# A mixture-of-experts kernel after linear attention: TensorE's order in the second expert job written by hand

## The chip, the cores and the metric

The kernel runs on one core of one Trainium2 chip. A core has five engines with instruction queues of their own: TensorE (PE in the profile; its weight loads are PEld), VectorE (DVE), ScalarE (ACT), GpSimd (POOL) and SyncE (SP, which here only issues transfers). Sixteen DMA engines move data between the device memory and the on-chip memories SBUF and PSUM. The metric is the time of one execution on the device in microseconds (us), the median of several runs.

## The reference, cut to what matters

```python
f = 1.0 / (1.0 + np.exp(-f_logit))                    # q, k, v, f_logit: 4 x 8 x 768 x 48
for t in range(S):
    state = f[:, :, t, :, None] * state + np.einsum('bhd,bhe->bhde', k[:, :, t], v[:, :, t])
    y[:, :, t] = np.einsum('bhd,bhde->bhe', q[:, :, t], state)
x = np.ascontiguousarray(y.transpose(0, 2, 1, 3)).reshape(B * S, H * D)   # 3072 x 384
...
probs = softmax(x @ w_gate); expert_idx = np.argmax(x @ w_gate, axis=1)   # 8 experts, 768 places each
h = np.maximum(np.einsum('ecd,edf->ecf', disp, w1), 0.0)                  # w1: 8 x 384 x 1024
y = np.einsum('ecf,efd->ecd', h, w2)                                      # w2: 8 x 1024 x 384
out[i] = gate_w[i] * y[expert_idx[i], pos[i]]
```

Each of the 3072 rows of the attention's result goes through the two weight matrices of one expert, with a Relu between, and is scaled by its gate.

## The kernel before, in words

**Stages.** Up to about 150 us the attention runs in slots, and its rows are written, sorted by expert, to a table `disp` in device memory. Then follow nine *jobs*, each a number of rows through the weights of one expert. Job 0, here the *first job* (256 rows of expert 0), has its first products inside the slots, and its second products are TensorE's last work there. The *second job* takes the 224 left-over rows of expert 0, with the same weights (`wsets[0]`). The *third job* is the largest of the other experts (448 rows, weights `wsets[1]`); the fourth to ninth follow by size (424, 408, 392, 376, 360 and 352 rows).

**A job.** Rows, weights and hidden values are held as a high part and a low part (`xh`/`xl`, `w1h`/`w1l`, `hh`/`hl`; `x0h`/`x0l` for the second job), since TensorE multiplies rounded fp32: each product is high·high + high·low + low·high. The *first products* (`hidden`, L758) run over the 8 tiles `ft` of 128 hidden columns, and for each over 3 slices `c` of 128 input columns: 9 matmuls per `ft`, 72 per job. ScalarE takes Relu into `hh` (L764), VectorE the rest into `hl` (L765). The *second products* run, for rows in blocks `kb` of 128, over `ft` with 3 matmuls each (`ffn2_rows`, L1019; jobs two and three, and the last ones) or with weights and rows exchanged (`ffn2`, L1253). For the second job that is two blocks, 48 matmuls. ScalarE scales the result by the gate into `yo` (L1023) and GpSimd scatters it to the output (L330).

**Rows turned.** Rows arrive as `xg` (rows on partitions) and must be turned. For jobs two and three TensorE does it: `prep_second` (L1137, two transposes per slice) and `prep` (L1223, four per slice). For the later ones `columns` copies the rows into planes (GpSimd L1193, ScalarE L1194), four transposing transfers follow (L1197), and `prep_columns` puts them together (GpSimd L1206, ScalarE L1207, L1211, VectorE L1212).

**Weights.** An expert's weights come in seven pieces, three of `w1` (512 KB each) and four of `w2` (384 KB), through three buffers `raw` (L123, L129). ScalarE copies a piece to the high part (L136); VectorE, or GpSimd for the `w2` of the third job, subtracts for the low part (L145). A buffer is free again after that.

**Gates.** `gates` (L989 to L1004) works out each row's gate and its place in the output: some nine small VectorE operations and two on ScalarE.

**What sets the order.** Each engine runs its queue in order. In the attention part TensorE's order is written out by hand (`manual_schedule`), the first job's second products with it; hooks there put `prep_second` between them, its third slice after the last `ft`. Then a flag (`slow_wide`, L1495) is read on every engine and a branch taken (L1496); behind it, in `sorted_jobs`, a scheduler sets the order of all engines from its own estimates, the program's order and a few hints (`issue_after`: not ahead of that instruction in program order). SyncE's queue holds: three pieces of `w1` of the third job; its rows `xg` (which wait until the filling rows, `disp<-zero,fill_at`, are in `disp`); its four pieces of `w2`; the fourth job's rows; the fourth job's `w1`; and so on.

## Time and profile before

| | |
|---|---|
| three runs | 372.09, 373.45, 375.27 us |
| median | 373.45 us |
| profiled execution, own time | 371.12 us |
| its span (first to last instruction) | 369.4 us |
| TensorE busy | 352.4 us, 95% of the span |
| VectorE, ScalarE, GpSimd busy | 243.7, 221.9, 168.0 us |

The profile is of one execution. Its times count from the start of the span; 1.7 us of its own time lie outside. A busy TensorE is not a TensorE at its peak: its instructions are pipelined, so the distance between two starts is its pace, and the length of one is longer than that.

### The profile page before, as it was taken

The page shows a single profiled execution, that of the slowest core. Times are in us where ns is not written, and L with a number is a line of the kernel's source. Part 1 is how long each engine was busy: PE and PEld are TensorE (multiplying, and loading weights), DVE is VectorE, ACT ScalarE, POOL GpSimd, SP SyncE. Part 2 cuts the span into 40 slices and gives each one's busy share as a digit, 9 for nine tenths or more (in the row PEclk, how much of TensorE's full clock was granted, in tenths as well). Part 3 has the DMA queues.
Part 4 walks back from the last instruction along what each step waited for, and adds up shares of the span by engine and source line. Part 5 has one row for each costly group of instructions (what it writes and reads, how often), then busy time and mean ns, then how long its engine had stood idle before and what let it go on. Part 6 is the DMA issues. An engine that isn't in the chain of part 4 may idle for free. (4 is left out here: it accounts for less than half of the span.)

```text
span 369.4 us, 10094 instructions
## 1 busy us (share of the span) xinstructions
PE 352.4 (95%) x3895; PEld 331.3 (90%) x3895; DVE 243.7 (66%) x538; ACT 221.9 (60%) x457; POOL 168.0 (45%) x282
## 2 busy tenths in 40 slices
PE   7899999999999999949999999999999999999994
PEld 6799888888888889848999899999999999999993
DVE  4998998978998947652385387566955857570310
ACT  3466667876876653435377585749749678491311
POOL 6765545774867673516503530305517326133012
PEclk9999999999999999998999999999999999999999
DMA  7999999989785432564646989798599798821001
GB/s 170 187 218 215 235 220 240 225 220 267 174 228 147 140 110 88 200 205 146 231 112 202 226 251 204 250 208 277 160 210 280 184 215 263 162 95 66 14 23 42
DMA packets 110569, 67.53 MB, mean 183 GB/s; under 512 B 92995, under 2 KB 105052, under 8 KB 110512
## 3 DMA queue, kind: packets, MB, share of 16 engines
q1 hardware_dynamic: 106784, 56.74, 62.5%
q0 software_dynamic: 3456, 9.96, 7.4%
q8 instruction: 32, 0.52, 0.6%
q14 instruction: 25, 0.20, 0.2%
q10 hardware_dynamic: 272, 0.10, 0.1%
HBM read 49.26 MB, written 11.21 MB: 164 GB/s over the span
## 5 line engine op out<-in xcount | busy, mean ns | idle before, releaser
L330 POOL DMA_INDIRECT out_dram<-yo,g_ti x29 | 30.6, 1056 | 59.1 <-ACT yo L1023 35.1
L438 POOL TENSOR_SCALAR_AFFINE_SELECT AT<-AT 128x512 f32<-128x512 f32 x48 | 29.5, 640 | 19.5 <-ACT AT L436 19.5
L1019 PE MATMUL psM<-w2h,hh 128*128 128x384 f32 (+3 forms) x112 | 37.9, 339 | 0.0
L1019 PE MATMUL psM<-w2l,hh 128*128 128x384 f32 (+3 forms) x112 | 37.5, 338 | 0.0
L1019 PE MATMUL psM<-w2h,hl 128*128 128x384 f32 (+3 forms) x112 | 37.4, 337 | 0.0
L136 ACT ACTIVATE w2h<-raw 128x768 fp32r<-128x768 f32 x32 | 26.9, 843 | 13.6 <-DMA raw<-in_moe_w_dram 13.5
L1253 PE MATMUL psM<-hh,w2h 128*128 128x424 f32 (+3 forms) x96 | 33.1, 345 | 0.0
L1253 PE MATMUL psM<-hh,w2l 128*128 128x424 f32 (+3 forms) x96 | 33.0, 344 | 0.0
L1253 PE MATMUL psM<-hl,w2h 128*128 128x424 f32 (+3 forms) x96 | 33.0, 344 | 0.0
L390 DVE TENSOR_TENSOR_SCAN Suf<-psF,direv 112x511 f32<-112x511 f32 x24 | 29.0, 1210 | 3.7 <-PE psF L370 3.7
L436 ACT ACTIVATE AT<-psA 128x512 f32<-128x512 f32 x48 | 26.4, 613 | 7.5 <-PE psA L430 3.4
L145 DVE TENSOR_TENSOR w2l<-raw,w2h 128x768 fp32r<-128x768 f32 x28 | 27.4, 980 | 4.8 <-ACT w2h L136 4.1
L145 DVE TENSOR_TENSOR w1l<-raw,w1h 128x1024 fp32r<-128x1024 f32 x21 | 26.9, 1282 | 5.3 <-ACT w1h L136 5.1
L1273 POOL COPY yo<-yq 128x384 uint16<-128x384 uint16 (+4 forms) x15 | 13.0, 915 | 36.8 <-DMA yq<-yp 36.8
L330 POOL DMA_INDIRECT disp<-rows,ri x24 | 24.9, 1036 | 10.0 <-issue 3.7
L404 DVE TENSOR_TENSOR_SCAN Rq<-psF,d 112x512 f32<-112x512 f32 x24 | 29.4, 1224 | 0.0
L136 ACT ACTIVATE w1h<-raw 128x1024 fp32r<-128x1024 f32 x24 | 25.2, 1056 | 6.1 <-DMA raw<-in_moe_w_dram 6.0
L430 PE MATMUL psA<-qT,kT 48*128 48x128 f32 x384 | 27.5, 280 | 0.6 <-DVE qT L419 0.6
L765 DVE SCALAR_TENSOR_TENSOR hl<-psA,hh 128x224 fp32r<-128x224 f32 (+8 forms) x26 | 13.8, 532 | 20.7 <-ACT hh L764 19.6
L563 ACT ACTIVATE rows<-psA 128x384 f32<-128x384 f32 x24 | 11.8, 492 | 24.6 <-PE psA L547 19.0
L526 PE MATMUL psY<-AT,ld_v 128*48 128x128 f32 (+1 forms) x384 | 26.0, 273 | 0.0
L430 PEld LDWEIGHTS psA<-qT,kT 48*128 48x128 f32 x384 | 24.1, 189 | 1.2 <-ACT kn L461 0.7
(258 smaller groups left out, 1023.9 us busy)
## 6 DMA issues: line engine op xcount, KB each, us to landing
raw<-in_moe_w_dram SPq DMA_DIRECT2D x24, 512.0 KB
raw<-in_moe_w_dram SPq DMA_DIRECT2D x32, 384.0 KB
ld_kq<-in_k_dram SPq DMA_DIRECT2D x24, 192.0 KB
ld_kq<-in_q_dram SPq DMA_DIRECT2D x24, 192.0 KB
ld_v<-in_v_dram SPq DMA_DIRECT2D x24, 192.0 KB
ld_f<-in_f_logit_dram SPq DMA_DIRECT2D x11, 384.0 KB
xg<-disp SPq DMA_DIRECT2D x4, 589.5 KB
xg<-disp SPq DMA_DIRECT2D x5, 393.0 KB
```

The costliest lines, as they stand in the source:

```text
L136: return nc.scalar.activation(hi, raw, AF.Copy)
L145: engine.tensor_tensor(lo[cs], raw[cs], hi[cs].bitcast(F32), op=ALU.subtract)
L330: ins = nc.gpsimd.indirect_dma_start(out=dst, out_offset=bass.IndirectOffsetOnAxis(ap=idx, axis=0), in_=rows, in_offset=None, bounds_check ...
L390: nc.vector.tensor_tensor_scan(out=_view(Suf[:R], m - 1, [[-1, m]]), data0=_view(F, m, [[-1, m]]), data1=_view(direv[:R], m - 1, [[-1, m]] ...
L404: nc.vector.tensor_tensor_scan(out=Rq[:R], data0=F, data1=d1[:R], initial=0.0, op0=ALU.mult, op1=ALU.max)
L430: nc.tensor.matmul(pas[s][:, p], kTs[n][r, p], qTs[n][r, p], start=True, stop=True)
L436: nc.scalar.activation(AT[:, s], pas[s], AF.Copy)
L438: nc.gpsimd.affine_select(AT[:, s], AT[:, s], pattern=[[0, NP], [1, C]], compare_op=ALU.is_ge, fill=0.0, base=0, channel_multiplier=-1)
L526: nc.tensor.matmul(py[b][64 * g : 64 * g + m, a, :], vt[:, 2 * p + s, :m], AT[:, s, p, :], start=(first(n) and a == 0), stop=(a == NP // 2 ...
L765: nc.vector.scalar_tensor_tensor(out=hl[:, :T], in0=ph[:, :T], scalar=0.0, in1=hh[:, :T].bitcast(F32), op0=ALU.max, op1=ALU.subtract)
L1019: nc.tensor.matmul(py[:n], x[:, ks], a[:, ft], start=(ft == 0 and m == 0), stop=(ft == FT - 1 and m == 2))
L1253: nc.tensor.matmul(pys[c][:, :T], a[:, ft, cs], x[:, :T], start=(ft == 0 and n == 0), stop=(ft == FT - 1 and n == 2))
```

## The change

It writes TensorE's order in the second job by hand, in a new function `second_job`, and moves what stands around it:

- The third slice of the second job's own rows is turned inside the branch, after the first three `ft` have had their products of slice 0 (27 of the 72 first products now run slice by slice over three tiles).
- The three `w1` splits of the third job stand behind the evictions `hh` of `ft` 2, 3 and 5; the second job's gates, before ahead of the branch, behind `ft` 4, in a pool of their own.
- All 72 first products run before the third job's rows are turned; the three turns (four transposes each) stand in the second row block of the second products, behind `ft` 1, 3 and 5.
- The third job's gates and the four `w2` splits (high parts on ScalarE, low parts on GpSimd) are issued behind the last turn.
- `yo` keeps its three buffers in this job, and its scatters no wait for the fills (`fills=False`). The fourth job's rows are asked for behind the second job in program order. SyncE's queue holds the same transfers in the same order.

```diff
--- before.py
+++ after.py
@@ -1006,7 +1006,7 @@
 
     out_ins, filling = [], []
 
-    def ffn2_rows(wt, hs, pr, T, fpool, hooks=None):
+    def ffn2_rows(wt, hs, pr, T, fpool, hooks=None, fills=True):
         w1h, w1l, w2h, w2l = wt
         gate, ti = pr[2:]
         for kb in range(-(-T // P)):
...
@@ -1136,18 +1134,15 @@
             for kb in range(T_FIRST[0] // P):
                 nc.tensor.transpose(pt[:, kb * P : (kb + 1) * P], xg0[:, kb, c * P : (c + 1) * P], ident)
             act = nc.scalar.activation(x0h[:, c], pt, AF.Copy)
-            with tc.issue_after(filling[0]):
-                dve = nc.vector.tensor_tensor(x0l[:, c], pt, x0h[:, c].bitcast(F32), op=ALU.subtract)
-        if c == DT - 1:
-            with tc.issue_after(act.ins), tc.issue_after(dve.ins):
-                pr1.extend((x0h, x0l) + gates(xg0, T_FIRST[0] // P, w0pool))
+            with tc.issue_after(filling[0]) if c < DT - 1 else ExitStack():
+                nc.vector.tensor_tensor(x0l[:, c], pt, x0h[:, c].bitcast(F32), op=ALU.subtract)
 
     row_loads = []
     load_second()
     with tc.manual_schedule(engines={mybir.EngineType.PE}):
         with tc.issue_after(marks["rank"].ins):
             ffn2_rows(
-                wsets[0], hs0, (None, None) + g0, T_FIRST[0], h0pool, {(0, 3): order_experts, (1, 6): lambda: prep_second(0, 1), (1, 7): lambda: prep_second(2)}
+                wsets[0], hs0, (None, None) + g0, T_FIRST[0], h0pool, {(0, 3): order_experts, (1, 6): lambda: prep_second(0, 1)}
             )
 
     actx.close()
@@ -1165,6 +1160,7 @@
         row_loads.clear()
         fpool = fctx.enter_context(tc.tile_pool(name="fpool", bufs=2, reuse_waits="tile"))
         hpool = fctx.enter_context(tc.tile_pool(name="hpool", bufs=1, reuse_waits="tile"))
+        spool = fctx.enter_context(tc.tile_pool(name="spool", bufs=1))
         rawpool = fctx.enter_context(tc.tile_pool(name="rawpool", bufs=3, reuse_waits="tile"))
         wpool = fctx.enter_context(tc.tile_pool(name="wpool", bufs=1, reuse_waits="tile"))
         wsets[1:] = [weight_tiles(wpool)]
@@ -1216,15 +1212,61 @@
             nb = -(-T // P)
             xh = fpool.tile([P, DT, TMAX], F32R, name="xh", bufs=1)
             xl = fpool.tile([P, DT, TMAX], F32R, name="xl", bufs=1)
-            for c in range(DT):
+            acts = []
+
+            def turn(c):
                 pt = psT.tile([P, 4 * P], F32, name="psT")
                 for kb in range(nb):
                     n = min(P, T - kb * P)
                     nc.tensor.transpose(pt[:, kb * P : kb * P + n], xg[:n, kb, c * P : (c + 1) * P], ident[:n, :n])
-                act = nc.scalar.activation(xh[:, c, :T], pt[:, :T], AF.Copy)
-                dve = nc.vector.tensor_tensor(xl[:, c, :T], pt[:, :T], xh[:, c, :T].bitcast(F32), op=ALU.subtract)
-            with tc.issue_after(act.ins), tc.issue_after(dve.ins):
-                gate, ti = gates(xg, nb, fpool)
+                acts.append(nc.scalar.activation(xh[:, c, :T], pt[:, :T], AF.Copy).ins)
+                acts.append(
+                    nc.vector.tensor_tensor(xl[:, c, :T], pt[:, :T], xh[:, c, :T].bitcast(F32), op=ALU.subtract).ins
+                )
+
+            return xh, xl, turn, acts
+
+        def second_job(pieces):
+            T = jobs[1][1]
+            pools = (psA, "psA"), (psM, "psM")
+            tile = lambda ft: pools[ft % 2][0].tile([P, TMAX], F32, name=pools[ft % 2][1])
+            pieces2, hs, begun = [], [], [tile(ft) for ft in range(3)]
+            w1h, w1l = wsets[0][:2]
+            for c in range(DT):
+                if c == 1:
+                    prep_second(2)
+                for ft, ph in enumerate(begun):
+                    fs = slice(ft * P, (ft + 1) * P)
+                    for n, (a, x) in enumerate(((w1h, x0h), (w1h, x0l), (w1l, x0h))):
+                        nc.tensor.matmul(
+                            ph[:, :T], a[:, c, fs], x[:, c, :T], start=(c == 0 and n == 0), stop=(c == DT - 1 and n == 2)
+                        )
+            for ft in range(FT):
+                if ft < len(begun):
+                    ph = begun[ft]
+                else:
+                    ph = tile(ft)
+                    hidden(wsets[0], x0h, x0l, T, ft, ph)
+                hs.append(hidden_out(ph, T, ft, hpool, TMAX))
+                if ft in (2, 3, 5):
+                    with tc.issue_after(hs[ft][2]):
+                        split_piece(pieces.pop(0), nc.vector)
+                    pieces2.append(weight_piece(wsets[jobs[2][2]], expert(2), rawpool, DT + len(pieces2)))
+                if ft == 4:
+                    with tc.issue_after(hs[ft][2]):
+                        gate, ti = gates(xg0, T_FIRST[0] // P, spool)
+            xg, T1 = xgs.pop(2), jobs[2][1]
+            pieces = pieces2
+            xh, xl, turn, acts = prep(xg, T1)
+            ffn2_rows(
+                wsets[0], hs, (None, None, gate, ti), T, fpool, {(1, 2 * c + 1): lambda c=c: turn(c) for c in range(DT)}, False
+            )
+            with tc.issue_after(acts[-2]), tc.issue_after(acts[-1]):
+                gate, ti = gates(xg, len(range(0, T1, P)), fpool)
+                for n in range(FT // 2):
+                    if n == len(pieces):
+                        pieces.append(weight_piece(wsets[jobs[2][2]], expert(2), rawpool, DT + n))
+                    split_piece(pieces[n], nc.gpsimd)
             return xh, xl, gate, ti
 
         def ffn1(wt, pr, T, hook, later, pools):
@@ -1286,13 +1328,8 @@
         yp = fpool.tile([P, DT, 2, 4 * P], U16, name="yp", bufs=1)
         nc.gpsimd.memset(yp[:, :, :, min(sizes[j - 2] for j in range(2, NE + 1) if j not in IN_ROWS) :], 0)
         xgs, made = {}, {}
-        for n in range(DT + FT // 2):
-            if n == DT:
-                xgs[2] = load_rows(expert(2), jobs[2][1])
-            with tc.issue_after(row_loads[-1]) if row_loads else ExitStack():
-                split_piece(weight_piece(wsets[jobs[2][2]], expert(2), rawpool, n), nc.vector if n < DT else nc.gpsimd)
-        pr = pr1
-        hook = None
+        pieces = [weight_piece(wsets[jobs[2][2]], expert(2), rawpool, n) for n in range(DT)]
+        xgs[2] = load_rows(expert(2), jobs[2][1])
 
         def load_ahead(j):
             if j < len(jobs):
@@ -1303,25 +1340,27 @@
             made[3] = columns(xgs.pop(3), jobs[3][1])
             load_ahead(4)
 
-        for j, (_, T, ws) in list(enumerate(jobs))[1:]:
-            if j == 2:
-                hook = 3, first_columns
-            else:
+        with tc.manual_schedule(engines={mybir.EngineType.PE}):
+            pr = second_job(pieces)
+        load_ahead(3)
+        hook = 3, first_columns
+        for j, (_, T, ws) in list(enumerate(jobs))[2:]:
+            if j > 2:
                 load_ahead(j + 2)
             later = None
-            if 1 < j < len(jobs) - 1:
+            if j < len(jobs) - 1:
                 into, e = wsets[jobs[j + 1][2]], expert(j + 1)
                 load_weights(into, e, rawpool)
                 later = lambda n, ins, into=into, e=e: load_later(into, e, rawpool, n, ins)
             if j == len(jobs) - 1:
                 with tc.issue_after(out_ins[-1]):
                     nc.gpsimd.drain()
-            hs = ffn1(wsets[ws], pr, T, hook, later, ((psA, "psA"), (psM, "psM")) if j < 2 else ((psA, "psA"), (psT, "psT"), (psM, "psM")))
+            hs = ffn1(wsets[ws], pr, T, hook, later, ((psA, "psA"), (psT, "psT"), (psM, "psM")))
             cur = pr
             if j + 1 < len(jobs):
                 T1 = jobs[j + 1][1]
-                pr = prep_columns(made.pop(j + 1), T1) if j + 1 in made else prep(xgs.pop(j + 1), T1)
-            if j > 1 and j + 2 in xgs:
+                pr = prep_columns(made.pop(j + 1), T1)
+            if j + 2 in xgs:
                 made[j + 2] = columns(xgs.pop(j + 2), jobs[j + 2][1])
             if j in IN_ROWS:
                 ffn2_rows(wsets[ws], hs, cur, T, fpool)
```

In the rows of order below, numbers behind a name tell buffers apart.

TensorE, at the end of the first job: `xg_85` are the second job's rows, `slow_wide` the flag of the branch. Before:

```order
L1019 MATMUL psM<-w2h,hh_3281 128x384
L1019 MATMUL psM<-w2h,hl_3282 128x384
L1019 MATMUL psM<-w2l,hh_3281 128x384
L1137 MATMUL psT<-ident,xg_85 128x128 x2
L1495 TENSOR_LOAD slow_wide
L1496 COMPARE_AND_BRANCH
L758 MATMUL psA<-x0h,w1h 128x224
L758 MATMUL psA<-x0l,w1h 128x224
L758 MATMUL psA<-x0h,w1l 128x224
```

and with the change:

```order
L1534 TENSOR_LOAD slow_wide
L1535 COMPARE_AND_BRANCH
L1241 MATMUL psA<-x0h,w1h 128x224
L1241 MATMUL psA<-x0l,w1h 128x224
L1241 MATMUL psA<-x0h,w1l 128x224
L1241 MATMUL psM<-x0h,w1h 128x224
L1241 MATMUL psM<-x0l,w1h 128x224
L1241 MATMUL psM<-x0h,w1l 128x224
L1241 MATMUL psA<-x0h,w1h 128x224
L1241 MATMUL psA<-x0l,w1h 128x224
L1241 MATMUL psA<-x0h,w1l 128x224
L1135 MATMUL psT<-ident,xg_85 128x128 x2
```

The flag's read has moved ahead of the two transposes, which now stand behind the branch and nine products, three for each of three tiles.

TensorE, at the turns of the third job's rows (`xg`, which comes by the transfer L1175). Before, between the seventh and the eighth `ft` of the second job:

```order
L758 MATMUL psM<-x0h,w1l 128x224
L1223 MATMUL psT<-ident,xg 128x128 x2
L758 MATMUL psA<-x0h,w1h 128x224
...
L758 MATMUL psA<-x0h,w1l 128x224
L1223 MATMUL psT<-ident,xg 128x128
L1223 MATMUL psT<-ident,xg 128x64
L1223 MATMUL psT<-ident,xg 128x128 x3
L1223 MATMUL psT<-ident,xg 128x64
L1019 MATMUL psM<-w2h,hh_8877 128x384
```

and with the change (96 rows are the second row block):

```order
L1019 MATMUL psM<-w2h,hh_8882 96x384
L1019 MATMUL psM<-w2h,hl_8883 96x384
L1019 MATMUL psM<-w2l,hh_8882 96x384
L1221 MATMUL psT<-ident,xg 128x128 x3
L1221 MATMUL psT<-ident,xg 128x64
L1019 MATMUL psM<-w2h,hh_8886 96x384
L1019 MATMUL psM<-w2h,hl_8887 96x384
L1019 MATMUL psM<-w2l,hh_8886 96x384
L1019 MATMUL psM<-w2h,hh_8904 96x384
L1019 MATMUL psM<-w2h,hl_8905 96x384
L1019 MATMUL psM<-w2l,hh_8904 96x384
L1221 MATMUL psT<-ident,xg 128x128 x3
```

The first turn, which stood ahead of nine first products and all 48 second products, now stands behind the 72nd first product and 30 second products.

GpSimd, from the third job's `w2` low parts on. Before:

```order
L145 TENSOR_TENSOR w2l<-raw,w2h 128x768 x4
L330 DMA out_dram<-yo,g_ti 3072x384
L1177 MEMSET xg 128x9
L330 DMA out_dram<-yo,g_ti 3072x384
L1193 COPY planes<-xg 128x3x384
```

and with the change:

```order
L330 DMA out_dram<-yo,g_ti 3072x384
L145 TENSOR_TENSOR w2l<-raw,w2h 128x768
L1173 MEMSET xg 128x9
L145 TENSOR_TENSOR w2l<-raw,w2h 128x768 x2
L330 DMA out_dram<-yo,g_ti 3072x384
L145 TENSOR_TENSOR w2l<-raw,w2h 128x768
L1189 COPY planes<-xg 128x3x384
```

One of the second job's two scatters to the output (L330) now stands ahead of the four, the other between the third and the fourth.

## Rows read from the trace of the kernel before

**Rows 1.** The page's first part: busy us of each engine.
```profile
PE 352.4 (95%) x3895; PEld 331.3 (90%) x3895; DVE 243.7 (66%) x538; ACT 221.9 (60%) x457; POOL 168.0 (45%) x282
```
**Rows 2.** Windows: stretch, length, busy of each engine, PEclk, DMA share, GB/s.
```profile
161.35:166.19 4.84, 0.00 (x0) 0.03 (x1) 2.12 (x4) 0.78 (x4) 0.00 (x0) 1.00 0.69 190
166.42:169.83 3.41, 3.41 (x17) 2.68 (x15) 0.53 (x2) 2.34 (x5) 1.41 (x1) 0.50 0.74 261
170.03:179.26 9.23, 9.23 (x54) 8.64 (x53) 3.70 (x14) 3.72 (x9) 6.77 (x6) 1.00 0.24 57
220.00:300.00 80.00, 80.00 (x439) 79.46 (x438) 54.34 (x95) 55.50 (x98) 25.87 (x28) 1.00 0.91 220
```
**Rows 3.** Waits of TensorE over the span: total, times, longest.
```profile
PE psT L1223 <- DMA xg<-disp: 4.8, 1, 4.8
```
**Rows 4.** Timeline of TensorE: start, length, instruction, [idle before <- releaser].
```profile
152.68 0.34 PE L1019 MATMUL psM<-w2l,hh 128*128 128x384 f32 x1
153.20 0.44 PE L1137 MATMUL psT<-ident,xg 128*128 128x128 f32 x2 [0.19 <-DVE x0l L1140]
154.08 0.34 PE L758 MATMUL psA<-x0h,w1h 128*128 128x224 f32 x1 [0.44 <-ACT x0h L1138]
...
161.07 0.27 PE L758 MATMUL psM<-x0h,w1l 128*128 128x224 f32 x1
166.19 0.46 PE L1223 MATMUL psT<-ident,xg 128*128 128x128 f32 x2 [4.84 <-DMA xg<-disp]
166.35 0.49 PE L758 MATMUL psA<-x0h,w1h 128*128 128x224 f32 x1
...
168.35 1.75 PE L1223 MATMUL psT<-ident,xg 128*128 128x128 f32 x6
170.03 0.44 PE L1019 MATMUL psM<-w2h,hh 128*128 128x384 f32 x1
...
174.87 0.69 PE L1223 MATMUL psT<-ident,xg 128*128 128x128 f32 x4
175.49 0.44 PE L1019 MATMUL psM<-w2l,hh 128*128 128x384 f32 x1
...
179.26 0.37 PE L758 MATMUL psA<-xh,w1h 128*128 128x448 f32 x1
...
193.83 0.34 PE L1019 MATMUL psM<-w2h,hh 128*128 128x384 f32 x1
...
289.46 0.34 PE L1253 MATMUL psM<-hl,w2h 128*128 128x392 f32 x1
```
**Rows 5.** Timeline of SyncE's queue: the transfers that it issues.
```profile
161.63 0.39 SPq L1175 DMA_DIRECT2D xg<-disp  x1
...
163.24 7.39 SPq L129 DMA_DIRECT2D raw<-in_moe_w_dram  x4
...
178.88 1.53 SPq L123 DMA_DIRECT2D raw<-in_moe_w_dram  x3
```
**Rows 6.** Timeline of ScalarE, around the second job's own rows.
```profile
153.68 0.38 ACT L1138 ACTIVATE x0h<-psT 128x256 fp32r<-128x256 f32 x1
```
**Rows 7.** Timeline of VectorE, at the second job and at later splits.
```profile
154.10 0.42 DVE L1140 TENSOR_TENSOR x0l<-psT,x0h 128x256 fp32r<-128x256 f32 x1 [0.62 <-ACT x0h L1138]
...
189.31 1.23 DVE L145 TENSOR_TENSOR w1l<-raw,w1h 128x1024 fp32r<-128x1024 f32 x1
...
203.16 0.57 DVE L1212 TENSOR_TENSOR xl<-x,xh 128x424 fp32r<-128x424 f32 x1
...
283.32 0.56 DVE L765 SCALAR_TENSOR_TENSOR hl<-psT,hh 128x392 fp32r<-128x392 f32 x1
...
308.90 2.28 DVE L145 TENSOR_TENSOR w1l<-raw,w1h 128x1024 fp32r<-128x1024 f32 x1
```
**Rows 8.** Timeline of GpSimd.
```profile
168.42 5.43 POOL L145 TENSOR_TENSOR w2l<-raw,w2h 128x768 fp32r<-128x768 f32 x3 [10.44 <-ACT w2h L136]
...
308.74 1.42 POOL L1206 COPY x<-xq 128x1056 uint16<-128x1056 uint16 x1
```

More of the change, by code (lines that the diff above doesn't have):

```diff
@@ L1021, in ffn2_rows @@
                     hooks[kb, ft]()
-            yo = fpool.tile([P, DM], F32, name="yo", bufs=2 if hooks else 3)
+            yo = fpool.tile([P, DM], F32, name="yo", bufs=2 if hooks and fills else 3)
             nc.scalar.activation(yo[:n], py[:n], AF.Copy, scale=gate[:n, kb : kb + 1])
-            with tc.issue_after(filling[-1]) if hooks and kb else ExitStack():
+            with tc.issue_after(filling[-1]) if hooks and fills and kb else ExitStack():
                 out_ins.append(scatter(out, ti[:n, kb : kb + 1], yo[:n], N - 1, ("out",)))
@@ L1122, in fill_rows @@
             filling.append(scatter(disp, fill_at[:, i : i + 1], zero[:, :W], NV * RPE - 1, ("disp", "second")))
-    pr1 = []
     def load_second():
```

## The prediction

> **What bounds the kernel now.** I read the page's first part, then the waits of TensorE, then its timeline around the second job, and last the queues that feed it. TensorE is busy for 352.4 of 369.4 us [rows 1], so only its idle time, its slow time and its own work can give anything. Its longest wait by far is one of 4.8 us, at the first transposes of the third job's rows, for the transfer of `xg` [rows 3]. The timeline shows its place [rows 4]: 63 of the second job's 72 first products start from 154.08 to 161.07, TensorE stands until 166.19, and then come two transposes, nine first products at a slower pace, the other transposes, and the second products up to 179.26. [...] From 220 to 300 TensorE has no gap (80.00 of 80) while the DMA engines are 91% busy. So the stretch from 154.08 to 179.26, 25.18 us, is where the change acts; what follows is one unbroken row of matmuls, in which time won is kept as long as what feeds it keeps up.
>
> **The stretch before, term by term** [rows 4]. 63 first products at (161.07 - 154.08)/62 = 0.1127 make 7.10. Idle, 161.18 to 166.19: 5.01. Two transposes 0.16. Nine products at half clock, 166.35 to 168.35: 2.00. Six transposes 1.68. From 170.03 to 179.26: 9.23, of which the last four transposes take 175.49 - 174.87 = 0.62 and the 48 second products 8.61. The sum is 25.18.
>
> **The turns moved.** The same transfer releases them. Its issue at 161.63 [rows 5] waits for filling rows, which the change doesn't touch; nothing in SyncE's queue ahead of it is moved, so I let it land where it did, just before 166.19. TensorE now does its 72 first products and 30 second products first. The 72 cost 72 x 0.1127 = 8.12 (full clock, since no gap goes ahead), the 30 cost 30 x 0.1755 = 5.27 (pace of the second products in rows 4: 8.61/48 is 0.179 with its slower start, and 0.1755 in the row's middle). From a start at 153.5 (below), with 0.35 for two transposes and a short wait, the first turn is reached at 167.2, about 1.0 us behind the landing. The wait of 5.01 is gone. What is late next is that landing itself, with 1.0 us to spare. The nine products lose the half clock: 2.00 - 1.01 = 0.99. The twelve transposes cost three times the 0.62 of a turn at full clock, 1.86 in place of 2.46: 0.60.
>
> **The second job's own third slice.** Before, its two transposes stand ahead of the branch and the first product waits for ScalarE's copy [rows 4]. From the transposes at 153.20, which waited for VectorE, to the first product are 0.88 us, with flag and branch inside. Now the read of the flag follows the last second product of the first job (started 152.68 [rows 4]), so I take the first product 0.55 earlier, at 153.53; the bounds are 0 (if the read of the flag sets the time by itself) and 0.55. The two transposes come back inside the branch: 2 x 0.13 = 0.25 at most, from 0.62 for four. Then ScalarE's copy, 0.38 [rows 6], and VectorE's `x0l`, 0.42 [rows 7], must be through. Both engines have entered the branch by about 154.5, I estimate, for the gates that held VectorE ahead of it are now behind it. Transposes end at about 154.8, `x0h` is there at 155.3 and `x0l` at 155.8; TensorE has nine more products (1.01) and gets to slice 2 at 155.8. That is a wait of 0 to 0.5; I take 0.1, since the two chains meet.
>
> **Splits, gates, `w2`.** ScalarE and VectorE are not behind TensorE here: between 161.35 and 166.19 they work 0.78 and 2.12 of 4.84 us [rows 2]. The `w1` splits move behind the evictions of `ft` 2, 3 and 5, so an eviction waits for one split (1.23 on VectorE [rows 7]) at most; TensorE alternates between two kinds of PSUM tile and has two tiles' time (2 x 1.01) before it needs the next. I price that at nothing; uncovered it would be 1.23 for each of the three. The second job's gates are needed only at the first `yo`, some 6 us later: nothing. The `w2` splits of the third job go behind its last turn. ScalarE starts them at about 172.6, GpSimd needs 5.43 for three [rows 8] and 1.8 for the fourth, with a scatter of 1.0 between: the last ends at about 182.0. TensorE reads it at the end of the third job's second products, which begin at 193.83 - 6.8 = 187.0: 5 us to spare at the start alone. But these splits free the `raw` buffers for the fourth job's `w1`, whose three transfers were issued from 178.88 to 180.4 [rows 5]: the last of them now waits for the fourth split, and is issued about 2.0 us later than before. Its split ended at 190.54 [rows 7], and the fourth job's first product comes at 193.83 + 96 x 0.1746 = 210.6, or 203.8 after the change; 192.5 against 203.8 leaves 11 us.
>
> **The sum.** 5.01 + 0.99 + 0.60 + 0.55 - 0.25 - 0.10 = 6.80 us. With the start at its bound of 0 it is 6.25, without wait and with the transposes hidden 7.15. The profiled execution took 371.12, so 364.3 (span 362.6). It is 2.3 us below the median of the runs shown, 373.45; against the median the forecast is 373.45 - 6.8 = **366.6**, its own range 365 to 368 with the spread of the runs. One per cent, about what a measurement of this kernel can tell from no change, is 3.7 us: the line is at 369.7.
>
> **Rival A: the feeding chain doesn't follow.** TensorE comes 6.8 us earlier to everything behind 172, the transfers, planes and splits do not all do so: with DMA engines at 91% [rows 2] a late start may stay late. The fourth job's last `xl` piece ended at 203.73 [rows 7] for products at 210.6, a cushion of 6.9 by itself; the smallest that I find later is that of the `hl` that ended at 283.88 and was read at 289.46 [rows 4, 7], 5.6 us. If the chain is pushed by the 2.0 us of the last `w1` transfer and gets nothing of the 6.8, the gain that is kept is 5.6 - 2.0 = 3.6, and the time 369.8. Against it: the fourth job's planes are copied by ScalarE behind an eviction of the third job, so they move with TensorE; and that `hl` is itself made from a product. I give it 0.13.
>
> A row bears on its size. The `w1l` split of VectorE that started at 308.90 took 2.28 us where that at 189.31 took 1.23 [rows 7], and GpSimd's copy into `x`, from 308.74, ran beside it for 1.42 [rows 8]. [...] It speaks against this change: the third job's gates read `xg` on VectorE and now run while GpSimd subtracts `w2l`. [...] In the trace before no gates ran beside the subtractions of 168.42 [rows 8].
>
> **Rival B: the rows land later.** The turn now has about 1.0 us to spare against a landing that rests on the fills. `xg`'s packets share the DMA engines with nothing new, but if the fills end later each us beyond 167.2 costs one, and a gap long enough to halve the clock another 1.7 (half of the 3.41 us at 0.50 [rows 2]). A landing 2 us later costs 1.0 + 1.7 at most: a gain of 4.1, 369.4. Chance 0.05.
>
> **Rival C, slower than before: the `raw` buffers.** The four subtractions on GpSimd, now behind the last turn, hold the three buffers; the fourth job's `w1` stands behind them in SyncE's queue, its rows' transposing transfers behind that, and everything later behind these. To be slower by 1% (3.7) TensorE would have to wait 10.5 us at the fourth job, so its last `w1` split would have to end at 203.8 + 10.5 = 214.3 where it ended at 190.54: 24 us later, for an issue that I put 2.0 us later. It decides from 203.8 on, 13 us late. Chance 0.02.
>
> **Rival D: it doesn't do what it says.** The order of TensorE's instructions shows turns and products where the diff puts them, so only a wait that I missed at a hand-set place (a PSUM tile still held by an eviction behind a split, when the order by hand can't run ahead) could keep the idle time: 5 us would be back, 6.8 - 5.0 = 1.8, 371.6. Chance 0.02.
>
> **How the numbers follow.** The main case has 0.78, A 0.13, B 0.05, C and D 0.02 each. The forecast is that of the main case, 366.6. Faster by over 1% are the main case, most of B and half of A: 0.78 + 0.05 + 0.07 = 0.90; C is slower, 0.02; the rest, 0.08, is within 1%. The range goes from 364.0 (the upper bound of the sum, 366.3, and the 2.3 us by which one execution lay below the median) to 370.0, which takes in A at 369.8.
>
> **What would show it.** In the profile of the changed kernel: no TensorE wait for `xg`, or one under 0.5 us, at the first turn near 167; no stretch with a granted clock of 0.50 between 153 and 180; first product of the second job near 153.5; a wait for `x0l` of at most 0.5 some 2 us later; second products ending near 172.4 in place of 179.26, and the third job's beginning near 187.0 in place of 193.83. Then no TensorE idle up to about 358. The last `w2l` of the third job should end near 182, the fourth job's last `w1` transfer be issued near 182. The forecast is wrong if there is a new wait of several us at the fourth job or later (A, C), if the landing moves (B), or if the second job's first products show gaps at the evictions (D).

## The result, and the profile after

The changed kernel took 369.53 us (median of 7 runs, 368.15 to 372.40), the kernel before 373.45 beside it (7 runs, 371.22 to 375.62): a ratio of 0.9899, interval 0.985 to 0.9949, or 3.9 us less. That is 0.5 us inside the upper end of the range forecast, and 2.9 us above the likeliest time, 366.6. The profiled execution took 369.53 with a span of 367.7.

The wait for `xg` [rows 3] is gone. What is longest in the second job now is this (waits of TensorE, columns as there):

```profile
PE psA L758 <- DVE hl L765: 0.8, 1, 0.8
```

Timeline of TensorE, for the rows of before in [rows 4]:

```profile
156.23 0.33 PE L1019 MATMUL psM<-w2l,hh 128*128 128x384 f32 x1
156.40 0.28 PE L1241 MATMUL psA<-x0h,w1h 128*128 128x224 f32 x1
156.76 0.37 PE L1241 MATMUL psA<-x0l,w1h 128*128 128x224 f32 x1
...
159.03 0.37 PE L1241 MATMUL psA<-x0h,w1h 128*128 128x224 f32 x1
159.48 0.37 PE L1241 MATMUL psA<-x0l,w1h 128*128 128x224 f32 x1
...
161.37 0.27 PE L758 MATMUL psM<-x0h,w1l 128*128 128x224 f32 x1
162.41 0.37 PE L758 MATMUL psA<-x0h,w1h 128*128 128x224 f32 x1 [0.77 <-DVE hl L765]
...
166.52 0.35 PE L1019 MATMUL psM<-w2h,hh 128*128 128x384 f32 x1
...
171.75 0.69 PE L1221 MATMUL psT<-ident,xg 128*128 128x128 f32 x4
...
176.07 0.69 PE L1221 MATMUL psT<-ident,xg 128*128 128x128 f32 x4
...
177.80 0.37 PE L758 MATMUL psA<-xl,w1h 128*128 128x448 f32 x1
...
191.71 0.34 PE L1019 MATMUL psM<-w2h,hh 128*128 128x384 f32 x1
```

Windows of it (columns as in [rows 2]): full clock from the first product to the third job, and a feed no worse than before.

```profile
156.40:166.52 10.12, 9.19 (x75) 8.56 (x75) 5.72 (x15) 6.03 (x15) 4.06 (x6) 1.00 0.72 227
166.52:177.80 11.28, 11.28 (x66) 10.12 (x65) 4.26 (x12) 3.08 (x7) 0.97 (x1) 1.00 0.55 178
...
220.00:300.00 80.00, 80.00 (x439) 79.53 (x438) 56.27 (x97) 56.16 (x97) 25.19 (x27) 1.00 0.93 216
```

Two things are to be seen in these two executions. From the start of the first job's last second product to the start of the third job's first one are 191.71 - 156.23 = 35.48 us, where before had 193.83 - 152.68 = 41.15 [rows 4]: 5.67 won of the 6.80 forecast. But the first of these two products starts 3.55 us later than before, though both kernels run the same instructions up to there. The part ahead of the branch, which the prediction left as it was, took back more than half.

Every profile of this study divides in the same way. "First" is the start of the first job's last second product, "third" that of the third job's first one, "stretch" the time between the two, "rest" the time from "third" to the end of TensorE's last product. All are in us; the last column says how long the granted clock was 0.50 within the stretch:

| kernel | first | third | stretch | rest | span | half clock in the stretch |
|---|---|---|---|---|---|---|
| before | 152.68 | 193.83 | 41.15 | 170.61 | 369.4 | 3.4 |
| changed | 156.23 | 191.71 | 35.48 | 170.66 | 367.7 | 0 |
| e6_before_again | 148.86 | 191.90 | 43.04 | 170.61 | 367.7 | 10.2 |
| e5_after_again | 151.72 | 185.78 | 34.07 | 170.66 | 361.6 | 0 |
| e1_tiles | 152.41 | 186.49 | 34.08 | 170.66 | 362.6 | 0 |
| e2_turns_first | 153.62 | 196.46 | 42.83 | 170.66 | 372.4 | 10.2 |
| e3_slice_ahead | 154.95 | 189.61 | 34.66 | 170.66 | 365.6 | 0 |
| e4_no_scatter | 152.74 | 186.83 | 34.09 | 170.66 | 363.1 | 0 |
| e7_tiles_early | 151.89 | 185.63 | 33.74 | 170.66 | 361.5 | 0 |
| e8_w2_early | 154.53 | 194.34 | 39.81 | 170.68 | 370.2 | 3.4 |
| e9_pad96 | 148.33 | 182.47 | 34.14 | 170.88 | 359.2 | 0 |
| e10_pad32 | 155.47 | 189.62 | 34.15 | 171.54 | 366.3 | 0 |
| e11_before_pad64 | 149.59 | 193.20 | 43.61 | 170.71 | 370.3 | 10.2 |
| e12_tiles_early_pad96 | 148.21 | 182.01 | 33.80 | 170.88 | 358.0 | 0 |

### The profile page after: what moved, and what is told of

Read it like the earlier page. It is cut to its first block, busy times and chain, and to the rows that moved or that the text cites. A ratio compares the mean times of both kernels' runs of the same rounds, so it can differ in the third digit from the quotient of the medians.

```text
span 367.7 us, 10099 instructions
## 1 busy us (share of the span) xinstructions
PE 354.2 (96%) x3895; PEld 332.5 (90%) x3895; DVE 246.5 (67%) x538; ACT 221.3 (60%) x457; POOL 167.9 (46%) x282
## 5 line engine op out<-in xcount | busy, mean ns | idle before, releaser
L330 POOL DMA_INDIRECT out_dram<-yo,g_ti x29 | 30.9, 1065 | 61.3 <-ACT yo L1023 44.4
L145 DVE TENSOR_TENSOR w2l<-raw,w2h 128x768 fp32r<-128x768 f32 x28 | 30.0, 1074 | 7.6 <-ACT w2h L136 6.1
L436 ACT ACTIVATE AT<-psA 128x512 f32<-128x512 f32 x48 | 26.3, 610 | 7.7 <-PE psA L430 3.6
L330 POOL DMA_INDIRECT disp<-rows,ri x24 | 24.8, 1033 | 10.1 <-issue 4.3
L145 DVE TENSOR_TENSOR w1l<-raw,w1h 128x1024 fp32r<-128x1024 f32 x21 | 25.8, 1230 | 1.9 <-ACT w1h L136 1.8
```

The costliest lines, as they stand in the source:

```text
L145: engine.tensor_tensor(lo[cs], raw[cs], hi[cs].bitcast(F32), op=ALU.subtract)
L330: ins = nc.gpsimd.indirect_dma_start(out=dst, out_offset=bass.IndirectOffsetOnAxis(ap=idx, axis=0), in_=rows, in_offset=None, bounds_check ...
L436: nc.scalar.activation(AT[:, s], pas[s], AF.Copy)
```

## The experiments

The first four experiments ran beside each other on one chip, the next four on a second and the last four on a third. Ratios are to the kernel before on the same chip, whose median was 370.23, 369.18 and 369.34 us. An eviction is the pair of steps by which ScalarE (`hh`) and VectorE (`hl`) take a finished product out of its PSUM tile; a mark is the signal by which TensorE tells another engine that a product is finished.

**e1_tiles.** The PSUM tiles of the first products in another order.

```diff
-            pools = (psA, "psA"), (psM, "psM")
-            tile = lambda ft: pools[ft % 2][0].tile(...)
+            pools = (psA, "psA"), (psM, "psM"), (psM, "psM")
+            tile = lambda ft: pools[ft % 3][0].tile(...)
```

> The second job's first products take their PSUM tiles in the order A, M, M in place of A, M, so that the tile of ft 4 and 5 is a free one and not the one whose eviction ends at 162.35 in the changed kernel. Theory (the missing 1.1 us of the forecast are mostly a wait for late evictions, and time won here is kept to the end): TensorE's wait of 0.77 us for hl goes, with the 0.1 of slower start behind it; the first products from 156.40 on take 9.2 in place of 10.1 us, and the time falls by 0.9 us, to about 368.6 where the changed kernel has 369.5. Rival (the jobs behind are fed too late by now, their smallest cushion being 1.8 us): the wait goes but turns up again later, and the time stays within 0.3 us of the changed kernel's.

Measured: 365.33 us, ratio 0.9867 (0.9792 to 0.9943). The wait is gone, and the stretch is 34.08, 1.4 less than in the changed kernel's first profile. But the tiles are not the cause: the changed kernel itself, in e5 below, has no such wait either.

**e2_turns_first.** The turns ahead of the second products, `for c in range(DT): turn(c)` in place of the hooks.

> The three turns of the third job's rows stand right behind the 72 first products, ahead of all second products; all else as in the changed kernel. Theory (most of the gain is that TensorE has work while the rows are on their way): the first turn is reached about 10.3 us behind the last second product of the first job, the rows land about 12.9 us behind it, so a wait of about 2.6 us for the transfer comes back; with the clock halved behind it up to 1.7 us more. 2.6 to 4.3 us slower than the changed kernel, 372.1 to 373.8, that is 0 to 1.3 us faster than before. Rival (the hand-set order as such, with fewer waits of the scheduler's kind, makes the gain, and the rows are fetched earlier when asked earlier): under 1 us slower than the changed kernel.

Measured: 373.58, ratio 1.0102 (1.0045 to 1.016): slower than before. Timeline and windows of it:

```profile
167.93 2.31 PE L1221 MATMUL psT<-ident,xg 128*128 128x128 f32 x8 [5.23 <-DMA xg<-disp]
```
```profile
168.00:175.50 7.50, 7.50 (x24) 5.96 (x25) 4.33 (x11) 4.07 (x8) 1.89 (x3) 0.50 0.33 117
```

The wait is all back, and longer than expected: the rows have landed 14.2 us behind the start of the first job's last product here, 13.3 in the changed kernel's first profile. With it comes the half clock, 10.2 us of it (165.3 to 175.6). The interleaving with the second products is what the gain rests on. The stretch is 42.83 where e5 has 34.07; this price of 8.8 us is twice the most that the theory had (4.3).

**e3_slice_ahead.** The hook `(1, 7): lambda: prep_second(2)` back, the call in `second_job` out.

> The third slice of the second job's own rows is turned ahead of the branch again; the products keep the order of the changed kernel. Theory (the slice inside the branch lets TensorE read the flag early, and costs the two short waits of 0.36 and 0.34 us and slow starts at slice 2): the flag is again read behind transposes that wait for VectorE, first product about 0.9 us behind the last transposes in place of 0.17 us behind the last product, a loss of about 1.2 us; the waits at slice 2 go, a gain of 0.7, and the evictions still come late. 0.3 to 0.8 us slower than the changed kernel. Rival (the slice inside the branch costs more than it brings, as the sum on record had it with 0.55 won and 0.35 lost at best): 0 to 0.7 us faster.

Measured: 367.21, ratio 0.994 (0.9899 to 0.9982); stretch 34.66, 0.6 more than e5. As the theory had it, TensorE waits ahead of the branch and behind it again:

```profile
155.47 0.44 PE L1135 MATMUL psT<-ident,xg 128*128 128x128 f32 x2 [0.19 <-DVE x0l L1138]
156.32 0.34 PE L1239 MATMUL psA<-x0h,w1h 128*128 128x224 f32 x1 [0.41 <-ACT yo L1023]
```

**e4_no_scatter.** `if not (hooks and fills and kb):` ahead of the scatter.

> Leaves out one scatter to the output: that of the second 128 rows of the first job, which GpSimd issues at 159.57 in the changed kernel, so 128 rows of the output are not written. Theory (TensorE's marks of finished products are held up while GpSimd issues a scatter: those of ft 0 to 2, whose products end from 159.97 to 160.64, all come at 161.43 to 161.61, and ScalarE's first eviction starts at 161.51): without this scatter the first eviction starts within 0.2 us of the end of ft 0's last product, and the wait of 0.77 us of TensorE at ft 4 falls under 0.2; 0.6 to 0.9 us faster than the changed kernel. Rival (ScalarE comes late of itself, from the branch or from three tiles that end together): first eviction still 1 us and more behind ft 0's last product, TensorE's wait stays at 0.6 to 0.9 us, time as the changed kernel's.

Measured: 366.27, ratio 0.9941 (0.9897 to 0.9985); stretch 34.09, no wait, first eviction on time. By itself it fits the theory. With e5 it says nothing, since there the scatter is in place and does no harm.

**e5_after_again**, no edit.

> The changed kernel itself, once more, on the chip of the next kernel. In its first profile TensorE's marks of finished products came up to 1.5 us late wherever GpSimd issued a scatter, ScalarE's first eviction started at 161.51, and TensorE waited 0.77 us at ft 4; in the profiles of the first four experiments no mark is late, also in those that keep that scatter. Theory (the late marks belong to the execution or its chip, not to the change): here the marks are on time, the wait is gone, and from the last second product of the first job to the third job's first second product are 34.1 us, as with the three tiles in turn and without the scatter, where the first profile had 35.48 and before 41.15. Rival (the order of the changed kernel brings the late marks about, and the three tiles or the missing scatter cured them): late marks, the wait and 35.5 us again. The stretch behind it to TensorE's last product is 170.66 in both cases.

Measured: 364.06, ratio 0.9877 (0.9832 to 0.9923); stretch 34.07. Timelines of ScalarE and of GpSimd in the first profile of the changed kernel, and in this one:

```profile
161.51 0.36 ACT L764 ACTIVATE hh<-psA 128x224 fp32r<-128x224 f32 x1 [2.54 <-PE psM L758]
```
```profile
159.57 0.97 POOL L330 DMA_INDIRECT out_dram<-yo,g_ti  x1 [0.30 <-DMA raw<-in_moe_w_dram]
```
```profile
155.19 0.36 ACT L764 ACTIVATE hh<-psA 128x224 fp32r<-128x224 f32 x1 [1.09 <-PE psA L1241]
```
```profile
154.97 0.97 POOL L330 DMA_INDIRECT out_dram<-yo,g_ti  x1 [0.30 <-issue]
```

The first two lines are of the first profile, the last two of this one. Both times `ft` 0's last product ends while GpSimd issues its scatter. In the first profile the eviction started 1.5 us behind the end of that product (159.69 + 0.28), here 0.1 us (154.81 + 0.28). The theory holds: the late marks do not come with the change, and the first profile of the kernel before has them too (last section).

**e6_before_again**, no edit.

> The kernel before, once more, on the same chip. Its first profile had the first job's last product end at 153.02, the changed kernel's at 156.56, though both run the same instructions up to there. Theory (that part differs from one execution to the next, by the transfers of the attention): here it is anywhere between 152 and 157, not tied to the kernel, and from there to the third job's second products are 41.1 us within 0.8. Rival (the change itself makes the part ahead of the branch 3.5 us longer): 153.0 within 0.5 here, and about 156.5 for the changed kernel beside it.

Measured: 368.95, ratio 0.9996 (0.9969 to 1.0023). The first part ended 3.8 us earlier than in the first profile (149.20), so it does vary; but the eight profiles of the changed kernel and of those made from it by then (the changed one, e1 to e5, e7 and e8) all ended it later than this, at 152.05 to 156.56. So neither theory had it right: the part varies, and it is also longer with the change. The last four experiments look for the reason. In both kernels it was longer in the first profile than in the repeat, by 3.8 us (before against e6) and 4.5 us (changed against e5), nearly all of it gathered between 77 and 140 us; the change's own share is 2.9 us between e5 and e6. The stretch was 1.9 longer here than in the first profile of before, by the clock. Windows:

```profile
157.50:162.19 4.69, 0.00 (x0) 0.03 (x1) 2.12 (x4) 1.77 (x4) 0.00 (x0) 0.77 0.68 182
...
162.40:168.00 5.60, 5.60 (x22) 4.75 (x22) 1.74 (x5) 4.05 (x8) 3.32 (x2) 0.50 0.56 186
```

The idle time was 4.7 us, about as before (4.84), but the granted clock was at 0.50 for 10.2 us, where the first profile had 3.4. The longer spell is the usual one: of the 27 runs of the kernel before beside e5 to e8, 21 had a mean granted clock of 0.983 or less (e6's profile has 0.982), and two had 0.993, as the first profile.

**e7_tiles_early.** e1's edit, and `(1, 5): lambda: prep_second(0, 1)`.

> The three tiles in turn, and the first two slices of the second job's own rows turned one ft earlier in the first job, so that their low parts are ready when the branch is through. In the changed kernel the second product of the second job waits 0.25 us for x0l, whose subtraction started 0.03 behind ScalarE's copy; the third slice costs about 0.15 more. Theory: the first wait goes, 0.3 us less than the 34.1 of the three tiles alone, 33.8; the rows of the third job then have 0.6 us to spare, and the end moves with it. Rival (the rows of the second job have not landed at the earlier place, or the rows of the third job come too late): a wait of TensorE for xg at the one or the other place, and no gain or a loss of up to 1 us.

Measured: 364.8, ratio 0.9913 (0.9873 to 0.9954); stretch 33.74. The 0.33 us expected are won there, but in the timed runs they are lost in the spread.

**e8_w2_early.** The loop over the four `w2` splits ahead of `prep(xg, T1)`, outside the two `issue_after`.

> The third job's four w2 splits come ahead of its turns in the program, without the hint that holds them back; ScalarE's queue then has them ahead of the copies of the turned rows, and the buffers for the fourth job's weights come free some 6 us earlier. Theory (nothing behind the third job is short of feed, but the copies of the turned rows are needed soon): the fourth piece waits for a buffer and its transfer, ScalarE's copies of the turned rows stand behind it, and TensorE waits 2 to 4 us at its first products of the third job; the time is 2 to 4 us more than the changed kernel's, and the earlier buffers bring nothing. Rival (the late buffers hold the later jobs up): TensorE loses under 1 us here and the time is the changed kernel's or less.

Measured: 371.52, ratio 1.0077 (1.0036 to 1.0118). Timelines of ScalarE and TensorE:

```profile
174.95 0.84 ACT L136 ACTIVATE w2h<-raw 128x768 fp32r<-128x768 f32 x1 [2.63 <-DMA raw<-in_moe_w_dram]
175.69 0.96 ACT L1222 ACTIVATE xh<-psT 128x448 fp32r<-128x448 f32 x2
```
```profile
176.27 0.50 PE L758 MATMUL psA<-xh,w1h 128*128 128x448 f32 x1 [3.95 <-ACT xh L1222]
```

The theory's wait came, 3.95 us, and 3.4 us of half clock behind it. Together they make the stretch 5.7 longer than e5's, more than the 2 to 4 expected. The rest is 170.68: earlier buffers bring nothing. The hint that holds these splits back is a needed part of the change.

**e9_pad96**, **e10_pad32**, **e11_before_pad64.** One unused tile, of 24, 8 and 16 numbers (4 bytes each), the last in the kernel before; the edit of e9:

```diff
     x0l = w0pool.tile([P, DT, T_FIRST[0]], F32R, name="x0l")
+    pad = w0pool.tile([P, 24], F32, name="pad")
+    nc.gpsimd.memset(pad[:, :1], 0.0)
```

> The changed kernel with an unused tile of 96 bytes a partition behind the second job's tiles, and nothing else. The change moved the second job's gates out of the pool that lies ahead of the attention's load tiles in SBUF, so these tiles start 608 bytes lower: at 83104 in place of 83712, 160 past a multiple of 256 where they were on one. In every profile of a kernel with that layout the 384-byte pieces of the attention's loads take 32 to 34 ns on average, in both of the kernel before 26; the first job's last product ends at 152.1 to 156.6 there, at 153.0 and 149.2 in the two of before. With the 96 bytes the tiles lie on a multiple of 256 again (83200). Theory (the place of the tiles costs the change some 3 us in its first 150 us): 26 ns, the first job done by about 149.5, the stretch from there still 34.1 us, and the time 2 to 4 us less than the changed kernel's 364.1, ratio to before about 0.978 to 0.983. Rival (that part differs by itself between executions, and the pieces are slow for another reason): 33 ns or no earlier end, and 364 again.

> The same with 32 bytes: the load tiles start at 83136, a multiple of 64, 192 past a multiple of 256. A piece of 384 bytes that starts on a multiple of 256 or in the middle between two lies in two stretches of 256; from a start 192 past one, every second piece lies in three, as in the changed kernel's layout. Theory (what costs is the number of 256-byte stretches that a piece touches): as slow as the changed kernel, 32 to 34 ns a piece, time within 1 us of 364.1. Rival (a multiple of 64 is enough): 26 ns, and the 2 to 4 us won as with 96 bytes.

> The kernel before with an unused tile of 64 bytes, so that its load tiles start at 83776, 64 past a multiple of 256; nothing of the change is in it. Theory (the layout alone makes the loads slow, with no part of the change's order): 32 to 34 ns a piece of 384 bytes in place of 26, the first job done 2 to 4 us later than in the kernel before beside it, and the time 2 to 4 us more than before, ratio 1.005 to 1.011. Rival (the loads are slow by something else in the changed kernel): 26 ns, and the time of before within 0.5 us.

Measured: e9 360.46, ratio 0.9767 (0.9715 to 0.9819); e10 366.82, 0.9929 (0.9893 to 0.9964); e11 370.25, 1.0025 (0.9993 to 1.0057). From 5 to 110 us the windows of e6, e5, e9, e10 and e11 read, in this order (the column after the clock is the DMA engines' busy share):

```profile
5.00:110.00 105.00, 102.02 (x2164) 91.61 (x2165) 95.87 (x186) 72.79 (x177) 67.44 (x148) 1.00 0.94 226
```
```profile
5.00:110.00 105.00, 100.48 (x2097) 90.59 (x2098) 94.09 (x183) 70.86 (x173) 64.99 (x143) 0.97 1.17 219
```
```profile
5.00:110.00 105.00, 103.46 (x2180) 93.60 (x2181) 96.04 (x186) 72.78 (x177) 67.90 (x150) 1.00 0.97 231
```
```profile
5.00:110.00 105.00, 98.21 (x2112) 88.21 (x2111) 94.58 (x184) 71.41 (x175) 65.53 (x145) 1.00 1.12 213
```
```profile
5.00:110.00 105.00, 99.89 (x2145) 89.35 (x2148) 95.58 (x186) 72.77 (x177) 66.58 (x148) 1.00 1.02 220
```

| load tiles start past a multiple of 256 | kernels | mean of a 384-byte packet, 0 to 110 us | of a 192-byte packet | first job done |
|---|---|---|---|---|
| 0 | before, e6, e9, e12 | 26.3, 25.7, 26.1, 26.4 ns | 16.3, 16.0, 16.4, 16.3 ns | 153.02, 149.20, 148.67, 148.55 |
| 64 | e11 | 29.2 ns | 17.3 ns | 149.93 |
| 160 | changed, e5 | 34.4, 33.9 ns | 20.2, 20.5 ns | 156.56, 152.05 |
| 192 | e10 | 33.0 ns | 19.7 ns | 155.81 |

96 bytes that nobody reads give 3.6 us (360.46 against e5's 364.06, on two chips where the kernel before is 0.2 apart), as the theory had it, and the packets are as quick as before. Part of what lies between the two profiles is the clock (e5's has 6.8 us at a granted clock of 0.50 from 11.7 us on, e9's none there), but not of what lies between the runs: five of e5's six have a mean granted clock of 0.998 or more and took 363.3 to 365.4 us, five of e9's six have the same and took 359.3 to 362.0.

A multiple of 64 is not enough: e10 has slow packets again (33.0 ns, e9 26.1) and is 6.4 us slower than e9 on the same chip. That is 2.7 above 364.1, where the theory had it within 1 us. The profiles show how slow loads reach TensorE. Its waits in e10 have at their head

```profile
PE psF L724 <- DMA xg<-disp: 3.2, 1, 3.2
PE psT L372 <- POOL kqp L413: 2.3, 3, 0.9
...
PE psA L494 <- DMA ld_v<-in_v_dram: 1.4, 1, 1.4
```

(the first job's rows, copies of loaded rows, loaded rows); none of the three is among e9's. Why the first is as long as 3.2 us in e10, and under 1 in the other profiles, is open.

e11 fell short of its expectation: 29.2 ns, and 0.9 us with an interval that includes no change. The expectations of e10 and e11 counted the 384-byte packets (`ld_kq`, `ld_f`), of which every second crosses one more multiple of 256 from a start at 64, 160 or 192. They left out the 192-byte packets (`ld_v`, one every 256 bytes), which cross none from 0 and 64 and one each from 160 and 192. With both kinds e11 has 18,432 more crossings than before, e10 and the changed kernel 43,008. Added up from the traces, all these packets together took 1,338 to 1,370 us in the four profiles from 0, 1,492 in e11, 1,690 in e10, 1,747 and 1,754 in e5 and the changed kernel: 7.2, 7.7, 9.0 and 9.2 ns for each crossing more. That the start of the tiles sets the packets' pace, and with it the time, is shown by e9 against e10. That the crossings are the rule is the author's guess: it fits, but no run separates it from others or shows that 256 bytes is the size that counts, and it does not say why a 384-byte packet itself takes 29.2 ns from 64 and 33.0 from 192.

**e12_tiles_early_pad96.** e7's edits and the 96 bytes.

> The 96 bytes, the three PSUM tiles in turn, and the first two slices of the second job's rows turned one ft earlier. Theory: 33.7 us from the first job's last product to the third job's second products, as with the two edits alone, and the first 150 us as with the 96 bytes: 0.3 us under the kernel with the 96 bytes alone, 2 to 4 us under the changed kernel, the fastest of all. Rival (with the first part earlier, the third job's rows come too late for the turns, which had 0.6 to 0.9 us to spare): a wait for xg of up to 1 us, and no gain over the 96 bytes alone.

Measured: 361.08, ratio 0.9774 (0.9735 to 0.9813), stretch 33.80; TensorE doesn't wait for the third job's rows. It has the shortest span of all, 358.0, but in the timed runs it is no better than e9: 0.3 us cannot be told apart there. Both are faster than the changed kernel (0.9877 in e5) and than the one before.

## Why the prediction was right, and where not

**The stretch was right, and its terms nearly.** The forecast for the changed kernel was 41.15 - 6.80 = 34.35; e5 has 34.07. The twelve transposes and 48 second products take 10.44 (10.47 forecast), the third job's 72 first products 14.72 (14.57). The largest departure is at the branch. The forecast took the first product 0.55 earlier than before, 0.85 behind the last second product's start; it follows by 0.17. The read of the flag, from 154.99 to 155.47 on TensorE's queue in the first profile, is over before that last product starts (156.23). That is 0.68 more than forecast. Against it stand 0.3 us in the first products: the wait for `x0l` at slice 2 was forecast at 0.1 and is inside the 0 to 0.5 allowed (159.03 to 159.48 in the first profile), but a second one at the second product (156.40 to 156.76) was not in the sum. e3 prices moving the slice at 0.6.

**The turns.** The landing had 1.0 us to spare by the forecast. Counted from the signal that the rows have landed it had 2.2 in the first profile, and 0.4 to 1.5 in the nine later ones with the turns in their new place. e2 shows that the wait was the term it was taken for. What it is worth is wider than the 5.01 + 0.99 + 0.60 of the sum, since that came from one profile whose slow clock (0.50 [rows 2]) lasted 3.4 us; where it lasts 10.2, the gain in the stretch is 43.04 - 34.07 = 9.0.

**"I price that at nothing"**, of the evictions behind the splits, was right in e5 and cost 0.9 us in the first profile (161.37 to 162.41, less the 0.11 of one product), by marks that came late, not by a split.

**The step that failed is the one that wasn't written.** The sum was subtracted from the whole time as if all that lies ahead of the branch stayed as it was. It does, instruction by instruction. But the gates' tiles moved to another pool, and all that lies above them in SBUF moved down by 608 bytes. The forecast read the order and never the addresses. This cost about 3.6 us (e9 against e5), half of what the order wins. The packets of 384 bytes that are written there took 34.4 ns on average in the first profile of the changed kernel, 26.3 in that of the kernel before; why a start elsewhere makes them slower, no run shows.

**What was luck.** The time is inside the range by 0.5 us, and the range reached that far to take in Rival A, which did not come. Two things that the sum left out pull opposite ways. The part ahead of the branch takes 2.9 to 3.6 us from the gain (e5 against e6, and the first two profiles), and the longer spell of slow clock, usual in the kernel before, adds 1.9 to it (43.04 against 41.15). Faster by over 1% was given 0.90; measured is 1.0%, with an interval from 0.5 to 1.5%, and 1.2% in e5.

**The rivals.** A, the feed, did not decide: the rest is 170.61 before and 170.66 after, and 170.88 in e9, with TensorE 11 us earlier than before at the third job. Only e10 has more, 171.54. A VectorE instruction that takes longer beside one of GpSimd, as the prediction read it from the split of 308.90 in [rows 7], did come in the third job's gates: `L1004` took 1.83 us where it had taken 0.16, and `L997` 1.27 where it had taken 0.19, both beside GpSimd's subtractions of `w2l`, which before had ended at 176.40. `L996` and `L999`, beside the same subtractions, took 0.35 and 0.19 as before; what sets the longer ones apart is not shown. That the subtractions are the cause is the author's estimate from these times; no run leaves them out. Timelines of VectorE before, then of VectorE and GpSimd in the changed kernel:

```profile
177.04 0.16 DVE L1004 TENSOR_SCALAR g_ti<-g_ti 128x4 int32<-128x4 int32 x1
177.92 0.19 DVE L997 TENSOR_TENSOR g_sp<-g_sp,g_sn 128x32 f32<-128x32 f32 x1
```
```profile
178.24 1.83 DVE L1004 TENSOR_SCALAR g_ti<-g_ti 128x4 int32<-128x4 int32 x1
180.66 1.27 DVE L997 TENSOR_TENSOR g_sp<-g_sp,g_sn 128x32 f32<-128x32 f32 x1
```
```profile
178.16 1.88 POOL L145 TENSOR_TENSOR w2l<-raw,w2h 128x768 fp32r<-128x768 f32 x1 [5.43 <-DVE g_m L989]
...
180.04 3.65 POOL L145 TENSOR_TENSOR w2l<-raw,w2h 128x768 fp32r<-128x768 f32 x2
```

TensorE waited for neither, and the sum has no term for them. B did not come: the rows landed 12.4 to 14.2 us behind the start of the first job's last product in the profiles with the change, 13.4 before, and TensorE waited for them in e2 alone, where the turns stood too early. C did not come either: the last `w2l` ended at 180.7 in e5, near the 182 forecast. D's place, the evictions, was where the first profile lost its 0.9.

## What to carry to other kernels

When a transfer is late by a fixed time, fill the engine's wait with work that it has anyway, and look at what the idle time costs beyond itself: here the slow clock behind it, 3.4 to 10.2 us at 0.50. Where an edit moves a tile to another pool, compare the addresses of everything above it as well as the order, above all of tiles that many small packets are written to: here 608 bytes took those of 384 bytes from 26 to 34 ns and cost 3.6 us, and 96 unused bytes put that back. And divide a profile at points that both kernels share: the part that cannot have changed is the first to look at when a sum is right and the time isn't.

## What the runs showed of the hardware

The start of the load tiles in SBUF set the pace of the packets written into them: e9 and e10 differ in the size of the unused tile alone, and their packets of 384 bytes took 26.1 and 33.0 ns on average, those of 192 bytes 16.4 and 19.7. At the four starts that were run the means are 25.7 to 26.4 and 16.0 to 16.4 ns (on a multiple of 256), 29.2 and 17.3 (64 past one), 33.9 to 34.4 and 20.2 to 20.5 (160), 33.0 and 19.7 (192). No run shows another start, or the reason. The DMA engines' busy share from 5 to 110 us went from 0.94 to as much as 1.17 with it; 1.17 is more than the 16 engines' time, so the times of packets overlap in this count.

In the first two profiles, of the kernel before and of the changed one, 57 and 53 of some 740 of TensorE's marks of finished products came over 0.3 us behind the end of their product, up to 2.8. Each of these products ended within 0.6 us of a scatter that GpSimd issued. In the later twelve profiles 0 to 5 marks were late. Neither kernel nor order explains that; what else differs between those two executions and the others is open. Most of the late marks lie between 52 and 143 us, where these two profiles also lost their 3.8 and 4.5 us against e6 and e5; that the marks are the cause of this loss is not shown.

The slow clock (0.50 granted) behind an idle time of TensorE of 4.7 to 5.2 us lasted 3.4 us in one execution (before) and 10.2 in three (e2, e6, e11). Behind waits of 3.9 us in e8 and 3.2 in e10 it lasted 3.4. In four executions the clock also fell within the first 37 us, for 3.4 to 10.2 us, without a wait as long as these.
